# Linear attention feeding a two-layer MLP on one core: moving the key-value products and attention matmuls of batches 1 to 3 within TensorE's order

## The chip, the cores and the metric

One core of a Trainium2 chip runs the whole program. The metric is the device time of one execution in microseconds, as the median of several runs. The profile is one further execution; its span runs from the first to the last instruction of the core, and the device time also holds what lies before and behind that.

## The reference

```python
q_s = exp(q - max(q, axis=-1)) ; q_s = q_s / (sum(q_s, axis=-1) + 1e-09)
k_s = exp(k - max(k, axis=2))  ; k_s = k_s / (sum(k_s, axis=2) + 1e-09)
kv  = einsum('bhsd,bhse->bhde', k_s, v)
x   = einsum('bhsd,bhde->bhse', q_s, kv)      # 8 batches, 8 heads, 576 rows, 64
x   = x.transpose(0, 2, 1, 3).reshape(4608, 512)
h   = x @ w_in                                # 512 -> 2048
out = maximum(0.01 * h, h) @ w_out            # 2048 -> 512
```

q is normalised over the 64 elements of a head, k over the 576 rows; each batch and head has a 64 x 64 product kv. All inputs are float32, each batch's q, k and v 1.18 MB.

## The kernel before

**Two streams of work.** TensorE runs the MLP over the 4,608 tokens in nine tiles t of 512. For every tile, layer 1 computes 16 groups ph (128 hidden features each) of four accumulating matmuls over the four feature blocks of xT, taken in the order 0, 2, 1, 3 (L452). ScalarE turns each ph into gj with the leaky ReLU (L461). Layer 2 then accumulates 16 matmuls over the hidden blocks j into pout, for each of four groups of 128 tokens (L473), and VectorE (in two groups of tile 1 ScalarE) copies pout to out_sb, which SyncE's queue stores. In tile 0 the four groups of tokens run interleaved: four matmuls for j = 0, four for j = 1, and so on, so four pout accumulate at once. In the later tiles one group ends before the next begins.

Between these matmuls stands the attention of the batches that later tiles need. A tile of 512 tokens and a batch of 576 rows do not line up: tile 1 takes the last 64 tokens of batch 0 and the first 448 of batch 1, tile 2 the rest of batch 1 and the first 384 of batch 2.

**Steps of one batch's attention.** k_tree, k_allmax: maximum over rows on VectorE. k_sub: subtract it, on POOL or VectorE (L195). k_exp: exponential on ScalarE into ke (L203). v_cast: v to bfloat16 in vb, in two halves, on ScalarE (L213) or POOL (L215). q_max, q_sub, q_exp, q_sum, q_norm: softmax of q into qe (L226 VectorE, L256 POOL, L264 ScalarE, L273 and L280 VectorE). kv: 36 matmuls of 64 rows, in 18 pairs that use the two halves of the array at once, first all of the first pair of heads, then of the second (L295); the first half of them reads the first v_cast, the second half the second. kd_make: reciprocal and two multiplies for each of kv's two PSUM tiles, on VectorE, into the block-diagonal weights kd (L310, L313). q turned: for batches 0 and 1 by TensorE transposes (L389) that ScalarE copies out into qT (q_keep, L404), for later batches by a DMA into qX. attend or attend_x: a matmul of kd with the turned q for one feature block and a part of the tokens (L412, L440), which ScalarE copies into xT (L422, L446).

**What sets the order.** Every engine runs its instructions in the order in which the program issues them. The MLP's loops call run(t, u) at fixed points, and at(t, u, ...) hangs attention steps there; steps at the same point run in the order in which they were hung. In tile 0, unit u from 32 on is layer 2 behind hidden block j = u - 32 (four matmuls). In later tiles u below 16 is layer 1's group u, and u = 16 + 4 tsub + i is layer 2's group tsub behind its matmul j = 4 i + 3, so 19, 23, 27 and 31 are ends of groups. An at with u over 31 counts on into the next tile. Where the last block of a group ends, its stores are issued ahead of the steps hung there.

**PSUM.** Six buffers (psB) are shared by ph, pkv, the transposes and the attends; two more (psO) hold pout. In tile 0 two of the six hold pout2, the third and fourth group of tokens, until their stores. A new tile takes the buffer that was given back first, so it waits for whoever read that buffer last.

**The lines that the change touches**: L582 to L594 hang batch 1's steps in tile 0; plan (L599) sets kvu (L609), the unit of kv and one less than that of kd_make, as o + 25, with o = 27 for batch 3; plan2 (L617) hangs batch 2's steps in tile 1. RA is rows 0 to 3 of the nine that each partition holds, RB rows 4 to 8; H0 and H1 are the head halves; XR splits the nine rows in five and four.

Of the kernel before, what the change touches and what calls it, by code (L numbers as in the profile page):

```python
# [25 lines left out]
def kernel(  # L26
# [9 lines left out]
    nc = tc.nc  # L36
# [49 lines left out]
    RA, RB = slice(0, 4), slice(4, R)  # L86
# [115 lines left out]
    def k_exp(b, hs):  # L202
        nc.scalar.activation(  # L203
            out=st[b]["ke"][:, :, hs].rearrange("p r h d -> p h r d"),
            in_=st[b]["k"][:, hs],
            func=AF.Exp,
        )

    def v_cast(eng, b, gg):
        o = vb2[b % 2][:, :, gg, 0:128].rearrange("p r (h d) -> p h r d", h=2)  # L210
        i = st[b]["v"][:, 2 * gg : 2 * gg + 2]
        if eng is nc.scalar:
            eng.copy(out=o, in_=i)  # L213
        else:
            eng.tensor_copy(out=o, in_=i)  # L215
# [47 lines left out]
    def q_exp(b, rs):  # L263
        nc.scalar.activation(  # L264
            out=st[b]["qe"][:, rs].rearrange("p r h d -> p h r d"),
            in_=st[b]["q"][:, :, rs],
            func=AF.Exp,
        )

    def q_sum(b, rs):  # L270
        n = rs.stop - rs.start
        qsum = small_pool.tile([P, n, HL], FP32, name="qsum")
        nc.vector.reduce_sum(out=qsum, in_=st[b]["qe"][:, rs], axis=AX.X)  # L273
        st[b]["qrec", rs.start] = qrec = small_pool.tile([P, n, HL], FP32, name="qrec")
        nc.vector.reciprocal(out=qrec, in_=qsum)

    def q_norm(b, rs):
        n = rs.stop - rs.start
        qes = st[b]["qe"][:, rs]
        nc.vector.tensor_tensor(  # L280
            out=qes,
            in0=qes,
            in1=st[b]["qrec", rs.start].unsqueeze(3).to_broadcast([P, n, HL, D]),
            op=ALU.mult,
        )


    def kv(b):

        pkv = [psB_pool.tile([P, 2, 130], FP32, name="pkv", tag=BANK_TAG) for _ in range(2)]  # L290
        for gg in range(2):
            for r in range(R):
                for hh in range(2):
                    rows = slice(hh * L, (hh + 1) * L)
                    nc.tensor.matmul(  # L295
                        pkv[hh][:, gg, 0:129],
                        lhsT=st[b]["ke"][rows, r, 2 * gg : 2 * gg + 2].rearrange(
                            "p h d -> p (h d)"
                        ),
                        rhs=vb2[b % 2][rows, r, gg, 0:129],  # L300
                        start=(r == 0),
                        stop=(r == R - 1),
                    )
        st[b]["pkv"] = pkv

    def kd_make(b):
        for hh in range(2):
            pkv = st[b]["pkv"][hh]
            krec = small_pool.tile([P, 2, 1], FP32, name="krec")
            nc.vector.reciprocal(out=krec, in_=pkv[:, :, 128:129])  # L310
            for hp in range(2):
                p0 = hp * D
                nc.vector.tensor_tensor(  # L313
                    out=kd2[b % 2][p0 : p0 + D, 2 * hh : 2 * hh + 2, p0 : p0 + D],
                    in0=pkv[p0 : p0 + D, :, p0 : p0 + D],
                    in1=krec[p0 : p0 + D].to_broadcast([D, 2, D]),
                    op=ALU.mult,
                )
# [66 lines left out]
    def q_transpose(b, r0, n):  # L385
        ps = psB_pool.tile([P, NB, n, L], BF16, name="psum_qt", tag=BANK_TAG)
        for rr in range(n):
            for gg in range(2):
                nc.tensor.matmul(  # L389
                    ps[:, gg::2, rr],  # L390
                    lhsT=st[b]["qe"][:, r0 + rr, 2 * gg : 2 * gg + 2].rearrange(
                        "p h d -> p (h d)"
                    ),
                    rhs=ident,
                    is_transpose=True,
                    start=(rr == 0 and gg == 0),
                    stop=(rr == n - 1 and gg == 1),
                )
        st[b]["ps", r0] = ps

    def q_keep(eng, b, r0, n, gs=slice(0, 4)):
        o, i = st[b]["qT"][:, gs, r0 : r0 + n], st[b]["ps", r0][:, gs]
        if eng is nc.scalar:
            eng.copy(out=o, in_=i)  # L404
        else:
            eng.tensor_copy(out=o, in_=i)

    def attend(b, gs, c0, n, eng):

        ps = psB_pool.tile([P, len(gs), n], FP32, name="po", tag=BANK_TAG)  # L410
        for i, g in enumerate(gs):
            nc.tensor.matmul(  # L412
                ps[:, i],
                lhsT=kd2[b % 2][:, g],
                rhs=st[b]["qT"][:, g].rearrange("c r l -> c (r l)")[:, c0 : c0 + n],
                start=True,
                stop=True,
            )
        step = gs[-1] - gs[0] if len(gs) == 2 else 1
        o = xT[:, gs[0] : gs[-1] + 1 : step, b * S + c0 : b * S + c0 + n]  # L420
        if eng is nc.scalar:
            eng.copy(out=o, in_=ps)  # L422
        else:
            eng.tensor_copy(out=o, in_=ps)  # L424
# [59 lines left out]
    def at(t, u, *fns):  # L484
        while t > 0 and u >= 32:
            t, u = t + 1, u - 32
        hooks.setdefault((t, u), []).extend(fns)
# [3 lines left out]
            fn()  # L491

    H0, H1 = slice(0, 2), slice(2, 4)

    def load_all(b):
        whole = [(ALLH, ALLR)]
        st[b]["k"] = load(k, b, "k_raw", whole)
        st[b]["q"] = load(q, b, "q_raw", whole)
        st[b]["v"] = load(v, b, "v_raw", whole)
# [80 lines left out]
    at(0, 15, lambda: q_max(1, RA), lambda: q_sub(nc.gpsimd, 1, RA))  # L580
    at(0, 15, lambda: q_max(1, RB), lambda: q_sub(nc.gpsimd, 1, RB))
    at(0, 29, lambda: k_exp(1, H1))  # L582
    at(0, 31, lambda: k_exp(1, H0), lambda: v_cast(nc.scalar, 1, 0))
    at(0, 33, lambda: q_exp(1, RA), lambda: q_sum(1, RA), lambda: q_norm(1, RA))
    at(0, 33, lambda: v_cast(nc.scalar, 1, 1), lambda: q_exp(1, RB))
    at(0, 38, lambda: kv(1), lambda: kd_make(1), lambda: q_sum(1, RB), lambda: q_norm(1, RB))
    at(0, 41, lambda: q_transpose(1, 0, 2), lambda: q_keep(nc.scalar, 1, 0, 2))
    at(0, 42, lambda: q_transpose(1, 2, 2), lambda: q_keep(nc.scalar, 1, 2, 2))
    at(0, 45, lambda: q_transpose(1, 4, 3), lambda: q_keep(nc.scalar, 1, 4, 3))
    at(0, 46, lambda: q_transpose(1, 7, 2), lambda: q_keep(nc.scalar, 1, 7, 2))  # L590
    for i in range(8):
        at(0, 47, lambda i=i: attend(1, [i // 2], 288 * (i % 2), 288, nc.scalar))


    XR = (slice(0, 5), slice(5, R))
# [3 lines left out]
    def plan(b, o):  # L599
        t = b - 2  # L600
        at(t, o, lambda: k_begin(b), lambda: q_begin(b), lambda: k_tree(b, ALLH))
        at(t, o + 3, lambda: k_allmax(b), lambda: k_sub(nc.gpsimd, b, ALLH))
        at(t, o + 7, lambda: q_max(b, ALLR), lambda: q_sub(nc.gpsimd, b, ALLR))
        at(t, o + 11, lambda: k_exp(b, ALLH))
        at(t, o + 12, lambda: v_cast(nc.gpsimd, b, 0), lambda: v_cast(nc.gpsimd, b, 1))
        at(t, o + 16, lambda: q_exp(b, ALLR))
        at(t, o + 18, lambda: q_sum(b, ALLR))
        at(t, o + 21, lambda: q_norm(b, ALLR))
        kvu, pu = o + 25, o + (33 if b == 3 else 34)  # L609
        at(t, kvu, lambda: kv(b))  # L610
        at(t, kvu + 1, lambda: kd_make(b))
        at(t, o + 22, lambda: q_turn(b))
        for i in range(8):
            at(t, pu + i // 2, lambda i=i: attend_x(b, i // 2, XR[i % 2], nc.scalar))


    def plan2():  # L617
        b = 2
        at(1, 0, lambda: k_begin(b), lambda: q_begin(b), lambda: k_tree(b, ALLH))
        at(1, 3, lambda: k_allmax(b))  # L620
        at(1, 6, lambda: k_sub(nc.vector, b, H0), lambda: k_sub(nc.vector, b, H1))
        at(1, 9, lambda: k_exp(b, ALLH))
        for rs in XR:
            at(1, 9, lambda rs=rs: q_max(b, rs), lambda rs=rs: q_sub(nc.gpsimd, b, rs))
        at(1, 13, lambda: v_cast(nc.gpsimd, b, 0), lambda: v_cast(nc.gpsimd, b, 1))
        for i, rs in enumerate(XR):
            at(1, (13, 16)[i], lambda rs=rs: q_exp(b, rs), lambda rs=rs: q_sum(b, rs), lambda rs=rs: q_norm(b, rs))
            at(1, (15, 17)[i], lambda rs=rs: q_turn(b, rs))
        at(1, 21, lambda: kv(b))
        at(1, 22, lambda: kd_make(b))  # L630
        for i in range(8):
            at(1, 28 + i // 2, lambda i=i: attend_x(b, i % 4, XR[i // 4], nc.scalar))

    plan2()
    for b in range(3, B):
# [89 lines left out]
```

## Time and profile before

| | us |
|---|---|
| median of the runs shown | 297.52 |
| other runs shown | 296.36 and 1044.59 |
| span of the profiled execution | 293.0 |
| TensorE matmuls busy in it | 278.8 |
| of these layer 1 (L452) and layer 2 (L473) | 127.1 and 129.1 |
| kv (L295), attends (L412, L440), transposes (L389) | 8.5, 3.4 + 9.8, 3.2 |
| ScalarE, VectorE, POOL busy | 150.8, 144.9, 85.6 |

Busy times of matmuls overlap, since a matmul is counted until its result is out while the next has long begun; the distance from start to start says more. A row of the timeline gives the start, the length, the engine, the line, the operation, the tiles and the count of a run of equal instructions; what stands in square brackets is the time that the engine had no instruction before it, and what ended that. PEld are weight loads, one ahead of each matmul. A few per cent of the matmul records are missing from a trace: here layer 2 has 592 weight loads and 580 matmuls, layer 1 640 and 626. The granted TensorE clock is 0.998 of full speed over the span.

### The profile page before, as it was taken

How to read it: one execution, taken by the hardware profiler on the slowest of the kernel's cores; microseconds unless marked ns; L12 is line 12 of the kernel's file. 1: busy time of each engine (PE TensorE's matmuls, PEld its weight loads, DVE VectorE, ACT ScalarE, POOL GpSimd, SP SyncE). 2: the span in 40 equal slices, each digit the busy share in tenths (PEclk: the TensorE clock that was granted, in tenths of full speed). 3: DMA queues.
4: the chain of work that ended last, by engine and by line, in shares of the span. 5: the costliest groups of instructions: out<-in, count | busy, mean ns of one | idle time of the engine just before them, and what ended most of it. 6: DMA issues, size and time to landing. Idle time of an engine off the chain costs nothing.

```text
span 293.0 us, 4255 instructions
## 1 busy us (share of the span) xinstructions
PE 278.8 (95%) x1634; PEld 139.1 (47%) x1661; DVE 144.9 (49%) x240; ACT 150.8 (51%) x272; POOL 85.6 (29%) x61
## 2 busy tenths in 40 slices
PE   6596999999999999999999999999999999999995
PEld 2265845444544455454445544544455444444443
DVE  3947957885491597189367455735440200110011
ACT  4956682777058605951695338532854066007500
POOL 4645280025029307802920292029300000000000
PEclk9999999999999999999999999999999999999999
DMA  7999999694729553874399138923141310131032
GB/s 258 307 211 387 247 191 400 160 345 152 135 55 326 196 116 91 273 266 88 70 326 276 36 72 289 294 55 72 38 81 38 72 36 1 38 72 36 0 72 73
DMA packets 36580, 45.76 MB, mean 156 GB/s; under 512 B 15952, under 2 KB 19280, under 8 KB 36560
## 3 DMA queue, kind: packets, MB, share of 16 engines
q1 hardware_dynamic: 33120, 41.16, 47.4%
q0 software_dynamic: 3280, 4.20, 8.2%
q8 instruction: 13, 0.21, 0.3%
q10 hardware_dynamic: 160, 0.13, 0.1%
q14 instruction: 7, 0.06, 0.1%
HBM read 36.70 MB, written 9.44 MB: 157 GB/s over the span
## 4 chain that ended last, share of the span: by engine, by line
PE 84%; DMA 3%; DVE 3%; ACT 2%; POOL 2%; issue 1%; POOLq 0%; ACTq 0%
PE pout L473 40%; PE ph L452 39%; DMA w_in_sb<-in_moe_w_in_dram 3%; PE pkv L295 3%; PE po L440 2%; POOL k_raw L195 1%; DVE t L162 1%; ACT vb L213 1%; DVE k_raw L356 1%; ACT xT L422 1%; PE psum_qt L389 1%; POOL w_in_sb L133 0%; ACT qe L264 0%; DVE xT L424 0%; DVE m L179 0%
## 5 line engine op out<-in xcount | busy, mean ns | idle before, releaser
L452 PE MATMUL ph<-xT,w_in_sb 128*128 128x512 bf16 (+1 forms) x626 | 127.1, 357 | 4.3 <-DMA w_in_sb<-in_moe_w_in_dram 1.9
L473 PE MATMUL pout<-w_out_sb,gj 128*128 128x512 bf16 (+2 forms) x580 | 129.1, 373 | 0.9 <-issue 0.5
L461 ACT ACTIVATE gj<-ph 128x512 bf16<-128x512 f32 x144 | 82.5, 604 | 58.5 <-PE ph L452 57.9
L452 PEld LDWEIGHTS <-w_in_sb 128*128 128x128 bf16 x640 | 62.0, 98 | 66.1 <-issue 5.5
L473 PEld LDWEIGHTS <-gj 128*128 128x128 bf16 x592 | 56.9, 98 | 61.6
L467 DVE COPY out_sb<-pout 128x512 f32<-128x512 f32 (+1 forms) x34 | 22.7, 675 | 90.7 <-PE pout L473 82.1
L195 POOL TENSOR_TENSOR k_raw<-k_raw,kall 128x2304 f32<-128x2304 f32 (+1 forms) x6 | 29.1, 4844 | 86.2 <-DVE kall L187 55.8
L273 DVE TENSOR_REDUCE qsum<-qe 128x36 f32<-128x2304 bf16 (+4 forms) x11 | 19.8, 1800 | 39.5 <-ACT qe L264 39.5
L256 POOL TENSOR_TENSOR q_raw<-q_raw,qmax 128x2304 f32<-128x2304 f32 (+4 forms) x11 | 31.1, 2839 | 23.5 <-DVE qmax L226 23.5
L446 ACT CAST xT<-po 128x320 bf16<-128x320 f32 (+1 forms) x48 | 16.8, 402 | 40.0 <-PE po L440 40.0
L203 ACT ACTIVATE ke<-k_raw 128x2304 bf16<-128x2304 f32 (+2 forms) x11 | 17.5, 1595 | 9.7 <-POOL k_raw L195 9.4
L280 DVE TENSOR_TENSOR qe<-qe,qrec 128x2304 bf16<-128x2304 bf16 (+4 forms) x12 | 21.1, 1758 | 0.4
L226 DVE TENSOR_REDUCE qmax<-q_raw 128x36 f32<-128x2304 f32 (+4 forms) x11 | 19.4, 1788 | 0.0
L264 ACT ACTIVATE qe<-q_raw 128x2304 bf16<-128x2304 f32 (+4 forms) x11 | 16.9, 1535 | 0.0
L215 POOL CAST vb<-v_raw 128x1152 bf16<-128x1152 f32 x12 | 13.4, 1151 | 0.0
L467 ACT COPY out_sb<-pout 128x512 f32<-128x512 f32 (+1 forms) x3 | 1.6, 549 | 17.5 <-PE pout L473 17.5
L162 DVE TENSOR_TENSOR t<-k_raw 128x1024 f32<-128x1024 f32 (+1 forms) x10 | 10.1, 1010 | 0.4 <-DMA k_raw<-in_k_dram 0.2
L324 PE MATMUL pout<-zero 128*128 128x512 bf16 x26 | 8.9, 469 | 1.4 <-POOL zero L101 1.3
L162 DVE TENSOR_TENSOR t<-t 128x256 f32<-128x256 f32 (+2 forms) x20 | 9.6, 478 | 0.7
L440 PE MATMUL po<-qX,kd 128*128 128x320 bf16 (+1 forms) x48 | 9.8, 286 | 0.1
L295 PEld LDWEIGHTS <-ke 64*128 64x128 bf16 x252 | 7.2, 93 | 3.2 <-ACT gj L461 1.7
L295 PE MATMUL pkv<-vb,ke 64*128 64x129 bf16 x252 | 8.5, 216 | 0.1
(55 smaller groups left out, 103.5 us busy)
## 6 DMA issues: line engine op xcount, KB each, us to landing
out_dram<-out_sb SPq DMA_DIRECT2D x70, 128.0 KB, 2.4
q_raw<-in_q_dram SPq DMA_DIRECT2D x7, 1152.0 KB, 8.2
v_raw<-in_v_dram SPq DMA_DIRECT2D x7, 1152.0 KB, 11.0
k_raw<-in_k_dram SPq DMA_DIRECT2D x6, 1152.0 KB, 5.8
k_raw<-in_k_dram SPq DMA_DIRECT2D x4, 576.0 KB, 5.6
w_in_sb<-in_moe_w_in_dram POOLq DMA_DIRECT2D x8, 256.0 KB, 7.4
w_out_sb<-in_moe_w_out_dram POOLq DMA_DIRECT2D x3, 512.0 KB, 12.2
v_raw<-in_v_dram SPq DMA_DIRECT2D x2, 576.0 KB, 7.4
```

The lines of the kernel that those rows point to most:

```text
L162: nc.vector.tensor_tensor(out=o, in0=i0, in1=i1, op=ALU.max)
L195: eng.tensor_tensor(out=ks, in0=ks, in1=st[b]["kall"][:, hs].unsqueeze(2).to_broadcast([P, n, R, D]), op=ALU.subtract,)
L203: nc.scalar.activation(out=st[b]["ke"][:, :, hs].rearrange("p r h d -> p h r d"), in_=st[b]["k"][:, hs], func=AF.Exp,)
L226: nc.vector.tensor_reduce(out=m, in_=st[b]["q"][:, :, rs], axis=AX.X, op=ALU.max)
L256: eng.tensor_tensor(out=qs, in0=qs, in1=st[b]["qmax", rs.start].unsqueeze(3).to_broadcast([P, HL, n, D]), op=ALU.subtract,)
L273: nc.vector.reduce_sum(out=qsum, in_=st[b]["qe"][:, rs], axis=AX.X)
L280: nc.vector.tensor_tensor(out=qes, in0=qes, in1=st[b]["qrec", rs.start].unsqueeze(3).to_broadcast([P, n, HL, D]), op=ALU.mult,)
L295: nc.tensor.matmul(pkv[hh][:, gg, 0:129], lhsT=st[b]["ke"][rows, r, 2 * gg : 2 * gg + 2].rearrange("p h d -> p (h d)"), rhs=vb2[b % 2][row ...
L452: nc.tensor.matmul(ph, lhsT=w_in_sb[:, cb, j * P : (j + 1) * P], rhs=xT[:, cb, c0 : c0 + n], start=(i == 0 and first), stop=(i == NB - 1 a ...
L461: nc.scalar.activation(out=o, in_=ph, func=AF.Prelu, alpha=LEAKY_SLOPE)
L467: copy(out=out_sb, in_=pout)
L473: nc.tensor.matmul(pout, lhsT=g_sb[j // 2][:, j % 2, tsub * P : (tsub + 1) * P], rhs=w_out_sb[:, j, os], start=(j == 0), stop=(j == NF - 1),)
```

## The change

Batch 1 (tile 0): kv and kd_make move from unit 38 to unit 41, directly ahead of the transposes; the first v_cast goes ahead of the second half of k_exp on ScalarE; q_sum and q_norm of RB go ahead of kd_make on VectorE; the four transposes gather at units 41 and 43 (from 41, 42, 45 and 46); the eight attends, all at unit 47 so far, go to units 45 (two), 46 (three) and 47 (three), with feature blocks in the order 0, 2, 1, 3. Batch 2 (tile 1): kv moves from unit 21 to 23, the end of a layer-2 group, kd_make from 22 to 24; the attends take the order 0, 2, 1, 3. Batch 3: kv moves from unit 20 of tile 2 to unit 19, the end of a group, and kd_make from 21 to 20. No instruction is added or taken away.

```diff
+    GS = (0, 2, 1, 3)
...
     at(0, 29, lambda: k_exp(1, H1))
-    at(0, 31, lambda: k_exp(1, H0), lambda: v_cast(nc.scalar, 1, 0))
+    at(0, 31, lambda: v_cast(nc.scalar, 1, 0), lambda: k_exp(1, H0))
     at(0, 33, lambda: q_exp(1, RA), lambda: q_sum(1, RA), lambda: q_norm(1, RA))
-    at(0, 33, lambda: v_cast(nc.scalar, 1, 1), lambda: q_exp(1, RB))
-    at(0, 38, lambda: kv(1), lambda: kd_make(1), lambda: q_sum(1, RB), lambda: q_norm(1, RB))
-    at(0, 41, lambda: q_transpose(1, 0, 2), lambda: q_keep(nc.scalar, 1, 0, 2))
-    at(0, 42, lambda: q_transpose(1, 2, 2), lambda: q_keep(nc.scalar, 1, 2, 2))
-    at(0, 45, lambda: q_transpose(1, 4, 3), lambda: q_keep(nc.scalar, 1, 4, 3))
-    at(0, 46, lambda: q_transpose(1, 7, 2), lambda: q_keep(nc.scalar, 1, 7, 2))
+    at(0, 33, lambda: v_cast(nc.scalar, 1, 1), lambda: q_exp(1, RB), lambda: q_sum(1, RB))
+    at(0, 41, lambda: kv(1))
+    at(0, 41, lambda: q_norm(1, RB), lambda: kd_make(1))
+    for r0 in (0, 2):
+        at(0, 41, lambda r0=r0: q_transpose(1, r0, 2), lambda r0=r0: q_keep(nc.scalar, 1, r0, 2))
+    for r0, n in ((4, 3), (7, 2)):
+        at(0, 43, lambda r0=r0, n=n: q_transpose(1, r0, n), lambda r0=r0, n=n: q_keep(nc.scalar, 1, r0, n))
     for i in range(8):
-        at(0, 47, lambda i=i: attend(1, [i // 2], 288 * (i % 2), 288, nc.scalar))
+        at(0, (45, 45, 46, 46, 46, 47, 47, 47)[i], lambda i=i: attend(1, [GS[i // 2]], 288 * (i % 2), 288, nc.scalar))
...
-        kvu, pu = o + 25, o + (33 if b == 3 else 34)
+        kvu, pu = o + (24 if b == 3 else 25), o + (33 if b == 3 else 34)
...
-        at(1, 21, lambda: kv(b))
-        at(1, 22, lambda: kd_make(b))
+        at(1, 23, lambda: kv(b))
+        at(1, 24, lambda: kd_make(b))
         for i in range(8):
-            at(1, 28 + i // 2, lambda i=i: attend_x(b, i % 4, XR[i // 4], nc.scalar))
+            at(1, 28 + i // 2, lambda i=i: attend_x(b, GS[i % 4], XR[i // 4], nc.scalar))
```

## The prediction

> **What bounds the kernel now.** I read the page first, then the timeline around each place that the diff touches, row by row. The page:
>
> ```profile
> span 293.0 us, 4255 instructions
> ...
> PE 278.8 (95%) x1634; PEld 139.1 (47%) x1661; DVE 144.9 (49%) x240; ACT 150.8 (51%) x272; POOL 85.6 (29%) x61
> ...
> PE 84%; DMA 3%; DVE 3%; ACT 2%; POOL 2%; issue 1%; POOLq 0%; ACTq 0%
> ```
>
> TensorE is the bound: 95% busy, 84% of the chain. The chain's other engines stand almost wholly before 24 us (untouched) or at batch 1 (35 to 55 us). Neither program has more matmuls than the other, so the change can only gain where TensorE now stands still, and lose where it makes it stand. I therefore looked for holes at each moved step. A 128x512 matmul starts every 0.216 us, a transpose every 0.056, a kv pair every 0.056 and a 288-column attend every 0.123 when nothing waits (starts in the timeline).
>
> Batch 1's kv (unit 38), timeline (start, length):
>
> ```profile
> 41.88 1.14 ACT L213 CAST vb<-v_raw 128x1152 bf16<-128x1152 f32 x1
> ...
> 42.28 1.48 PE L295 MATMUL pkv<-vb,ke 64*128 64x129 bf16 x36
> ...
> 43.07 0.51 PEld L295 LDWEIGHTS <-ke 64*128 64x128 bf16 x17 [0.24 <-issue]
> ...
> 43.69 2.27 PEld L473 LDWEIGHTS <-gj 128*128 128x128 bf16 x12
> 43.92 2.54 PE L473 MATMUL pout<-w_out_sb,gj 128*128 128x512 bf16 x11 [0.16 <-issue]
> ```
>
> It takes 1.48, elsewhere 1.20: the second half waits for the second v cast, which ends at 43.02. That hole is 0.28 us and real. The "0.16 <-issue" behind it is not: there are 12 weight loads for 11 matmuls, so one matmul record is missing. The same at batch 2's kv (mid-group) beside batch 4's (at a group's end already):
>
> ```profile
> 73.81 1.20 PE L295 MATMUL pkv<-vb,ke 64*128 64x129 bf16 x36
> ...
> 74.94 0.55 PEld L473 LDWEIGHTS <-gj 128*128 128x128 bf16 x4
> 75.17 0.59 PE L473 MATMUL pout<-w_out_sb,gj 128*128 128x512 bf16 x2 [0.16 <-issue]
> ```
> ```profile
> 128.61 1.20 PE L295 MATMUL pkv<-vb,ke 64*128 64x129 bf16 x36
> ...
> 129.73 0.33 PEld L473 LDWEIGHTS <-gj 128*128 128x128 bf16 x3
> 129.74 0.60 PE L473 MATMUL pout<-w_out_sb,gj 128*128 128x512 bf16 x2
> ```
>
> The first weight load comes 1.13 (74.94-73.81) and 1.12 (129.73-128.61) after kv's start: the same. At batch 4 the matmul starts 0.01 behind its load; at batch 2 the record at about 74.94 is lacking and the one at 75.17 is the second.
>
> Batch 1's attends (all at unit 47) and layer 1 behind them, then batch 2's:
>
> ```profile
> 52.48 1.96 PE L412 MATMUL po<-qT,kd 128*128 128x288 bf16 x8
> ...
> 52.80 2.52 ACT L422 CAST xT<-po 128x288 bf16<-128x288 f32 x8 [0.40 <-PE po L412]
> ...
> 54.28 6.00 PE L452 MATMUL ph<-xT,w_in_sb 128*128 128x512 bf16 x25
> ...
> 55.38 4.63 PEld L452 LDWEIGHTS <-w_in_sb 128*128 128x128 bf16 x22 [0.29 <-issue]
> ```
> ```profile
> 84.56 1.54 PE L452 MATMUL ph<-xT,w_in_sb 128*128 128x512 bf16 x4
> 84.66 0.65 ACT L446 CAST xT<-po 128x256 bf16<-128x256 f32 x2 [0.43 <-PE po L440]
> ...
> 85.08 0.74 PEld L452 LDWEIGHTS <-w_in_sb 128*128 128x128 bf16 x4 [0.42 <-issue]
> ```
>
> Eight attends in a row need eight PSUM evictions on ScalarE (one each 0.29), and layer 1 needs their results. From the first attend (52.48) to the second layer-1 group (55.59) pass 3.11 us; the work is 8 x 0.123 + 4 x 0.216 = 1.84. Hole: 1.27 us. Batch 2: layer 1's second matmul takes feature block 2, evicted last but one; it starts at 85.08, 0.52 after 84.56 in place of 0.22. Hole: 0.30.
>
> **Part by part.**
> Batch 1's kv to unit 41. The last matmul of unit 38 starts at 41.97; 12 more put the last of unit 41 at 44.56, kv 0.31 later at 44.87 (as 41.97 to 42.28). ScalarE does the second v cast after q_exp RA, which waits for POOL (q_sub RA ends 40.65): 40.68, cast 41.64 to 42.78. The wait is gone by 2 us: -0.28. The swap of v cast and k_exp fills ScalarE's wait for POOL (0.84 at 38.81) and costs nothing; kv needs k_exp (40.1) only at 44.87.
>
> Group ends of batches 2 and 3: the entry into kv costs 0.31 from matmul start to kv start in both kinds of place (73.50 to 73.81, 128.30 to 128.61), the exit 0.15. I take 0; read literally, the idle rows would give 0.16 to 0.22 each. Trainium skill, "TensorE: Matmul & The Clock Gate", Part 3: a weight load overlaps a running matmul only where their row groups differ. By that rule, entry and exit of the half-array kv cost the same between any two full-array matmuls, group end or not, so it speaks against a gain here; with the restored records the trace agrees, and its sum would be mine.
> Their inputs: batch 3's kv comes 0.86 earlier (102.2), its v casts end at 97.6 and k_exp at 93.8. Batch 2's kd_make falls 1.7 later, to about 78.4; its first reader is the attend at 81.0, and VectorE has nothing else to do until 80.33.
>
> Ahead of transposes (batch 1): kv's exit into a transpose is not in the trace; kv into another matmul is 0.15 (13.69 to 13.84), into an attend 0.18 (15.81 to 15.99), a transpose into kv 0.24. I take 0.15, bounds -0.05 to +0.1 on it.
>
> New wait. VectorE now does q_sum and q_norm of RB before kd_make, and PSUM has six buffers, two in pout2. In the built program the first transpose of unit 43 takes the buffer of pkv's first half and waits for that half's two kd multiplies. When? q_exp RA 40.68, +1.08 q_sum; its chain to the next instruction takes 1.25 + 0.29 + 1.14 (42.01 to 44.69 before), so q_sum RB starts at 44.45 (its input, q_exp RB, ends 44.24 as before). These rows give the rest:
>
> ```profile
> 44.69 0.16 DVE L310 RECIPROCAL krec<-pkv 128x2 f32<-128x2 f32 x1
> 44.89 0.59 DVE L313 TENSOR_TENSOR kd<-pkv,krec 64x128 bf16<-64x128 f32 x2
> ...
> 46.34 1.49 DVE L273 TENSOR_REDUCE qsum<-qe 128x20 f32<-128x1280 bf16 x1
> ...
> 48.17 1.49 DVE L280 TENSOR_TENSOR qe<-qe,qrec 128x1280 bf16<-128x1280 bf16 x1
> ```
>
> 46.34 to 48.17 is 1.83, q_norm to its successor 1.41, kd's half 0.79 (44.69 to 45.48): 44.45 + 1.83 + 1.41 + 0.79 = 48.48. TensorE: kv's last pair 45.85, transposes 46.00, eight of them 0.45, eight matmuls 1.73: 48.18 wanted, 48.58 possible (0.05 for the semaphore, 0.05 to load). Stall +0.40; bounds 0 (VectorE half a microsecond sooner) and +1.0 (as much later). Queued behind it on TensorE: everything.
>
> Attends over units 45, 46, 47 (2, 3, 3). After the stall unit 45 is at 50.89; qT's last copy ends about 50.4, kd's second half about 49.3. The evictions run beside layer 2: the groups at 50.89, 52.00 and 53.23 wait for nothing. Layer 1 starts at 53.60; in order 0, 2, 1, 3 its third matmul needs the sixth eviction (done 53.96 + 0.05, wanted 54.03) and its fourth the eighth (54.56 + 0.05, wanted 54.25): 0.36 of the 1.27 stay, so -0.91 (bounds -0.6 and -1.27). Output copies, and with them batch 2's k_tree on VectorE, fall some 0.75 later. k_exp of batch 2 stood at 64.05 with its input done at 62.33, so that is covered; without that cover each 0.1 delays ScalarE by as much, behind six PSUM buffers.
>
> Batch 2's attends in order 0, 2, 1, 3: block 2 is there, the third matmul waits for 85.03 + 0.05 in place of 85.00, the fourth ends 0.06 late: hole 0.14 in place of 0.30, -0.15 (bounds 0 and -0.30).
>
> Sum: -0.28 + 0 + 0.40 - 0.91 - 0.15 = -0.94 us; span 292.1. From there TensorE has no wait that this could run into, so it reaches the end. The median shown, 297.52, is 4.5 us above the profiled span, the lowest run, 296.36, 3.4. So 295.4 to 296.6 for the same spread; I name 296.2.
>
> **Rivals.**
> (a) Group ends do save: the idle rows are time. For: "0.16 <-issue" three times, always mid-group. Against: the load counts, and holes of 0.43 every 10.8 us all through the trace, where nothing can wait. Gain 0.94 + 3 x 0.2 = 1.5: 295.6. Chance 7%.
> (b) Slower: the wait of unit 43's transposes for kd_make eats it all. Each microsecond that VectorE comes later costs one; from a stall of 1.34 (kd half at 49.4) the kernel is slower than before. For: two reductions and a multiply now stand ahead of it, with the qT copies and attends behind. Against: all five durations are rows. With 2.0: +0.66, 298.2. Chance 8%.
> (c) The same stall cools the clock: the first nine warm-up matmuls start every 0.43 (half speed) until 5.1 us, so one fall costs some 1.9 us; but after 1.85 us of idleness (6.2 to 8.1) matmuls again start every 0.22. It needs more than 1.85: about 2 + 1.9 - 1.34 = +2.6, 300.1. Chance 2%. The Trainium skill, same page, "Why this matters for your kernels", puts the limit at gaps of about 3 us; no run here shows it.
> (d) No change: the stall and the attends' remains cancel the gain to within 0.3, 297.4. Chance 13%.
> My forecast has 70%.
>
> **Numbers.** 2% is 6 us, about what a measurement of this kernel can tell from no change. All cases lie within it: same 0.96. Faster needs six times the gain; slower needs a mishap three times (c): 0.02 each. The range takes the lowest run less 1.3 (attends and vb gain whole, no stall), 295.1, to the median with case (d) and a little of (b), 297.7.
>
> **What would show it.** kv of batch 1 in 1.20 instead of 1.48 at 44.9; a TensorE hole of about 0.4 ahead of the L389 matmuls near 48.5, released by VectorE's L313; attends in groups of 2, 3, 3 without holes; second layer-1 group of the second tile near 54.8 (55.59 before); batch 2's second layer-1 matmul 0.22 after the first; 36 kv matmuls of batches 2 and 3 still in 1.13 plus the same entry and exit. A span change over 2 us either way would make it wrong.

## The result and the profile after

| | us |
|---|---|
| before, median of 22 runs | 296.10 |
| changed, median of 22 runs | 294.93 (293.68 to 295.61) |
| ratio, 95% interval | 0.996 (0.9944 to 0.9976) |
| span of the profiled execution, before and changed | 293.0 and 293.0 |

The kernel is 0.4% faster, 1.2 us by the medians and 0.7 to 1.7 us by the interval. The forecast change was 0.94 us. The forecast time, 296.2 in a range of 295.1 to 297.7, was nevertheless missed, by 0.2 us below the range: the level that the sum was put on was too high. In every run whose own span is on record, of either kernel and of all variants, the time is 1.72 to 1.85 us above that span. One run of the kernel before took 1044.59 us, which nothing on record explains; without it the median is 296.06.

The two spans are equal although the kernel is faster. The page of the changed kernel says where that goes:

```profile
span 293.0 us, 4282 instructions
...
PEclk9989999999999999999999999999999999999999
```

One slice of the granted clock, the third (14.7 to 22.0 us), is an 8. The timeline of TensorE alone from 13 us on, changed kernel (start, length, operation, count):

```profile
13.21 0.85 PE L365 MATMUL pkv<-vb,ke 64*128 64x129 bf16 x18 [1.45 <-ACT vb L213]
13.99 1.89 PE L324 MATMUL pout<-zero 128*128 128x512 bf16 x4
```

and of the kernel before:

```profile
13.22 0.69 PE L365 MATMUL pkv<-vb,ke 64*128 64x129 bf16 x18 [1.44 <-ACT vb L213]
13.84 1.04 PE L324 MATMUL pout<-zero 128*128 128x512 bf16 x3
```

Both programs are the same there. In the changed kernel's execution the matmuls run at half speed from 13.60 to 17.01 us (the 128x512 matmuls of that stretch start every 0.427 us in place of 0.216). Batch 1's kv starts at 45.84 us; with the same program up to there and a clock that held ("batch 1 alone" below) it starts at 44.87, 0.97 earlier. The view by stage gives the granted clock as the third number from the end, 0.52 here, since its window begins 0.12 us ahead of the half-speed stretch:

```profile
13.47:16.89 3.42, 3.42 (x34) 1.93 (x30) 1.57 (x5) 1.93 (x3) 1.78 (x3) 0.52 1.13 211
```

From 40 us on the two traces compare without it. Changed kernel, batch 1:

```profile
45.84 1.20 PE L295 MATMUL pkv<-vb,ke 64*128 64x129 bf16 x36
...
46.97 0.62 PE L389 MATMUL psum_qt<-ident,qe 128*128 128x128 bf16 x8
47.26 1.49 DVE L280 TENSOR_TENSOR qe<-qe,qrec 128x1280 bf16<-128x1280 bf16 x1
...
47.40 1.07 ACT L404 COPY qT<-psum_qt 128x512 bf16<-128x512 bf16 x2 [2.18 <-PE psum_qt L389]
...
48.87 0.59 DVE L313 TENSOR_TENSOR kd<-pkv,krec 64x128 bf16<-64x128 f32 x2
...
49.61 0.72 PE L389 MATMUL psum_qt<-ident,qe 128*128 128x128 bf16 x10 [0.29 <-DVE kd L313]
...
51.89 0.41 PE L412 MATMUL po<-qT,kd 128*128 128x288 bf16 x2
...
53.00 0.53 PE L412 MATMUL po<-qT,kd 128*128 128x288 bf16 x3
...
54.23 0.53 PE L412 MATMUL po<-qT,kd 128*128 128x288 bf16 x3
...
54.60 0.81 PE L452 MATMUL ph<-xT,w_in_sb 128*128 128x512 bf16 x3
55.61 0.81 PE L452 MATMUL ph<-xT,w_in_sb 128*128 128x512 bf16 x3 [0.20 <-ACT xT L422]
```

kv takes 1.20 in place of 1.48. The transposes of unit 43 wait for L313, kd_make's first half: the matmul ahead of them starts at 48.94, they at 49.61, 0.67 later, of which 0.22 is that matmul's own time and 0.46 the hole (the bracket shows 0.29, since the record of the last matmul reaches into the hole). At 49.16, when TensorE could have started them, q_norm (L280, to 48.75) and ScalarE's copies of the first transposes (L404, to 48.47) were done; kd_make's first half ends at 49.46. The attends stand in three groups without a hole. Layer 1's fourth matmul starts 0.58 after the third: a hole of 0.36. Batch 2, layer 1 of tile 2 behind its attends:

```profile
84.80 1.38 PE L452 MATMUL ph<-xT,w_in_sb 128*128 128x512 bf16 x5
...
85.31 0.10 PEld L452 LDWEIGHTS <-w_in_sb 128*128 128x128 bf16 x1 [0.20 <-issue]
```

Its third matmul comes 0.30 after the second and its fourth 0.27 after the third: holes of 0.08 and 0.06 where there was one of 0.30. Sum over what changed, from single starts: batch 1 from unit 38's last matmul to the second layer-1 group took 13.62 us and takes 12.88 (the changed trace has that matmul at 42.94 and the group at 55.82), batch 2 saves 0.16. Together -0.90; with +0.97 from the clock, +0.07, which is the difference of the spans (292.97 and 293.04).

### The profile page after: what moved, and what is told of

It reads as the page before. It is cut to its first block, busy times and chain, and to the rows that moved or that the text cites. A ratio compares the mean times of both kernels' runs of the same rounds, so it can differ in the third digit from the quotient of the medians.

```text
span 293.0 us, 4282 instructions
## 1 busy us (share of the span) xinstructions
PE 282.1 (96%) x1661; PEld 139.9 (48%) x1661; DVE 145.6 (50%) x240; ACT 150.7 (51%) x272; POOL 85.4 (29%) x61
## 4 chain that ended last, share of the span: by engine, by line
PE 85%; DVE 6%; POOL 2%; ACT 2%; issue 1%; POOLq 0%
PE pout L473 39%; PE ph L452 39%; PE pkv L295 2%; PE po L440 2%; DVE qe L280 1%; DVE qsum L273 1%; POOL k_raw L195 1%; DVE t L162 1%; PE pout L324 1%; PE psum_qt L389 1%; POOL q_raw L256 1%; PE po L412 1%; ACT xT L422 1%; PE pkv L365 1%; ACT qe L264 1%
## 5 line engine op out<-in xcount | busy, mean ns | idle before, releaser
L256 POOL TENSOR_TENSOR q_raw<-q_raw,qmax 128x2304 f32<-128x2304 f32 (+4 forms) x11 | 31.1, 2836 | 25.8 <-DVE qmax L226 25.8
L280 DVE TENSOR_TENSOR qe<-qe,qrec 128x2304 bf16<-128x2304 bf16 (+4 forms) x12 | 21.7, 1807 | 0.4
L324 PE MATMUL pout<-zero 128*128 128x512 bf16 x27 | 10.5, 536 | 1.3 <-POOL zero L101 1.3
L313 DVE TENSOR_TENSOR kd<-pkv,krec 64x128 bf16<-64x128 f32 x28 | 8.1, 289 | 0.7
```

Of the source, the lines that this page charges most:

```text
L256: eng.tensor_tensor(out=qs, in0=qs, in1=st[b]["qmax", rs.start].unsqueeze(3).to_broadcast([P, HL, n, D]), op=ALU.subtract,)
L280: nc.vector.tensor_tensor(out=qes, in0=qes, in1=st[b]["qrec", rs.start].unsqueeze(3).to_broadcast([P, n, HL, D]), op=ALU.mult,)
```

## The experiments

All edits are against the changed kernel unless it says before. Times are medians; "before" in each row is the kernel before on the same chip. "Layer 2" is the time from layer 2's first matmul to its last, start to start, in the profiled execution; it leaves the start out and holds all that the change moves on TensorE. In the kernel before it is 253.16 us, in the changed kernel 252.27.

| | runs | us | before | ratio (95%) | layer 2 |
|---|---|---|---|---|---|
| group ends alone | 1 | 297.47 | 295.14 | | 253.17 |
| batch 1 alone | 1 | 294.04 | 295.14 | | 252.42 |
| one transpose tile | 12 | 293.95 | 295.14 | 0.9963 (0.9941 to 0.9986) | 251.85 |
| attends 3, 4, 1 | 1 | 293.53 | 295.14 | | 251.90 |
| before, more warm-up | 11 | 294.43 | 294.79 | 0.998 (0.9964 to 0.9997) | 253.17 |
| more warm-up | 11 | 293.55 | 294.79 | 0.9949 (0.9933 to 0.9965) | 252.25 |
| one tile and 3, 4, 1 | 12 | 294.10 | 294.79 | 0.9962 (0.9939 to 0.9985) | 251.50 |
| all three | 5 | 292.84 | 294.79 | 0.9928 (0.9903 to 0.9953) | 251.48 |
| v_cast swap undone | 1 | 295.56 | 296.02 | | 252.50 |
| first warm-up row alone | 12 | 294.53 | 296.02 | 0.9963 (0.9943 to 0.9984) | 252.27 |
| second warm-up row alone | 12 | 294.28 | 296.02 | 0.9949 (0.993 to 0.9967) | 252.25 |

A single time says little here, since executions of one kernel lie up to 3 us apart. The kernels with one run are read by their traces. The last column says where the spread arises: the three kernels at 253.16 to 253.17 differ by 3.2 us in their spans (292.5 to 295.7), and the changed kernel agrees with its three warm-up variants to 0.03. What follows layer 2's last matmul takes 3.66 to 3.71 us in all thirteen profiles. So the spread lies ahead of layer 2, and the change is worth 0.89 to 0.92 us behind that point.

**Are the group ends worth anything?** The kernel before with only

```diff
-        kvu, pu = o + 25, o + (33 if b == 3 else 34)
+        kvu, pu = o + (24 if b == 3 else 25), o + (33 if b == 3 else 34)
...
-        at(1, 21, lambda: kv(b))
-        at(1, 22, lambda: kd_make(b))
+        at(1, 23, lambda: kv(b))
+        at(1, 24, lambda: kd_make(b))
```

> The kernel before with only the key-value products of batches 2 and 3 (and their kd_make) moved to the group ends. My theory: nothing, since the 0.16 us of idle behind a mid-group kv is a missing matmul record; from the last matmul ahead of kv to the first attend of its batch the distance is 1.44 us for kv plus 0.216 for each layer-2 matmul, mid-group or not, and the layer-2 loop of tiles 1 and 2 takes as long as before. Rival (the idle rows are time): 0.2 us less for each of the two.

Batch 2's kv and what follows, group ends alone:

```profile
78.25 1.20 PE L295 MATMUL pkv<-vb,ke 64*128 64x129 bf16 x36
79.38 4.49 PE L473 MATMUL pout<-w_out_sb,gj 128*128 128x512 bf16 x19
...
87.28 1.54 PE L452 MATMUL ph<-xT,w_in_sb 128*128 128x512 bf16 x5
```

No idle bracket any more, as hoped, and 19 records for the 20 matmuls between kv and the attends. What decides is a distance with the whole of kv in it. From the fourth layer-1 matmul of tile 1 to the first of tile 2, start to start, it is 29.190 us in the kernel before (55.374 to 84.564) and 29.191 here (58.087 to 87.278). From there to the last matmul ahead of batch 4's kv, which takes in batch 3's, it is 43.734 in both. The group ends are worth nothing, to 0.001 us in this execution. The theory holds, the rival falls. The span of 295.7 is the start's: this execution had two half-speed stretches, from 8.7 and from 25.8 us.

**Batch 1 alone.** Batches 2 and 3 back in their old places and order.

> The changed kernel with batches 2 and 3 put back to their old places and order. My theory: from the last matmul of unit 38 to the second layer-1 group of tile 1 it takes 12.9 us as in the changed kernel (13.6 before), with a hole of 0.46 ahead of unit 43's transposes and 0.36 in layer 1; batch 2's attends leave their old hole of 0.30 in layer 1 of tile 2; kv of batches 2 and 3, mid-group, costs 1.44 plus any matmul whose record is missing. Rival: 1.67 with all matmul records there.

From unit 38's last matmul (41.97) to the second group (54.85) it is 12.88 us, the hole ahead of unit 43's transposes is 0.46, layer 1's 0.36, batch 2's 0.30: all as expected. kv of batches 2 and 3 shows 1.67 from matmul to matmul again, with a record missing once more:

```profile
73.08 1.19 PE L295 MATMUL pkv<-vb,ke 64*128 64x129 bf16 x36
...
74.20 0.76 PEld L473 LDWEIGHTS <-gj 128*128 128x128 bf16 x5
74.43 0.81 PE L473 MATMUL pout<-w_out_sb,gj 128*128 128x512 bf16 x3 [0.16 <-issue]
```

The rival could have pointed to this row; the distances above answer it.

**What does unit 43 wait for?**

```diff
-    for r0 in (0, 2):
-        at(0, 41, lambda r0=r0: q_transpose(1, r0, 2), lambda r0=r0: q_keep(nc.scalar, 1, r0, 2))
+    at(0, 41, lambda: q_transpose(1, 0, 4), lambda: q_keep(nc.scalar, 1, 0, 4))
```

> The changed kernel with the four rows of RA transposed into one PSUM tile and copied out at once, so one PSUM buffer is free for the transposes of unit 43 and only the second of them (4 matmuls) takes the buffer that kd_make frees. My theory (the wait is for the buffer that kd_make's first half gives back): the hole ahead of unit 43's first transpose goes (0.46 to 0), 0.1 us stays ahead of the second, the kernel is 0.35 us faster than the changed one, 0.9957 to 0.993 of the kernel before. Rival (the transposes wait for q_norm of RB or for ScalarE's copies): the hole stays at 0.46.

```profile
48.66 0.59 DVE L313 TENSOR_TENSOR kd<-pkv,krec 64x128 bf16<-64x128 f32 x2
...
48.94 0.76 PE L389 MATMUL psum_qt<-ident,qe 128*128 128x128 bf16 x10
```

The transposes start while kd_make's first half still runs, 0.22 behind the matmul ahead of them: the first hole is gone, and 0.04 is left ahead of the second set (ten transposes take 0.60 in place of 0.56). So it was the buffer that kd_make frees and not q_norm or a copy. From unit 41's last matmul (45.32) to layer 1's fourth (54.98) it is 9.66 us, in the changed kernel 10.08 (45.53 to 55.61): 0.42 less. The times could not show that by themselves: the ratio, 0.9963, lies just above the expected stretch, and its interval holds the changed kernel's 0.996 too. One correction to the section on the kernel belongs here: a new tile does not take the buffer that comes free first in time. In the changed kernel the copies out of the first two transposes were done at 48.47, a microsecond before kd_make's first half, and the next transposes still waited for the latter. In the program kd_make stands ahead of those copies; whether that order decides, or a fixed turn of the buffers, no run here shows.

**What is left of the attends' hole?**

```diff
-        at(0, (45, 45, 46, 46, 46, 47, 47, 47)[i], ...
+        at(0, (45, 45, 45, 46, 46, 46, 46, 47)[i], ...
```

> The changed kernel with the eight attends at units 45 (three), 46 (four) and 47 (one). My theory (what stays of the attends' hole is the eviction of the last attend, behind two others): the hole of 0.36 us in layer 1 of tile 1 falls to 0.05 or less and the attends themselves wait for nothing. Rival (the hole comes from the output copies or from the return to layer 1): it stays at 0.36.

```profile
52.18 0.65 PE L412 MATMUL po<-qT,kd 128*128 128x288 bf16 x4
52.67 1.03 PE L473 MATMUL pout<-w_out_sb,gj 128*128 128x512 bf16 x4
53.53 0.29 PE L412 MATMUL po<-qT,kd 128*128 128x288 bf16 x1
53.65 2.54 PE L452 MATMUL ph<-xT,w_in_sb 128*128 128x512 bf16 x10
```

Layer 1's first groups run without a hole. With one attend directly ahead of layer 1 instead of three, the last eviction is ready in time: the fourth matmul starts 0.22 behind the third (0.58 in the changed kernel).

**Where do the two groups of times come from?** The kernel before, and the changed kernel, with nine more warm-up matmuls:

```diff
-    wake(14)
+    wake(17)
...
     k_all_pe(0, 1)
-    wake(2)
+    wake(8)
```

> The kernel before with nine more warm-up matmuls in the start (three more in the first row of them, six more ahead of the first key-value products), so TensorE stands idle less before 16 us. My theory (the two groups of times, some 1.2 us apart, come from the TensorE clock falling to half for one window of 3.4 us in the start of some executions): the times draw together around the lower group of the kernel before, 294.5 to 295.1. Rival (the spread has nothing to do with the start): the same two groups as before, about 294.8 and 296.2.

> The changed kernel with the same nine warm-up matmuls. My theory: one group of times around 293.9, 0.9 us below the kernel before with the same warm-up matmuls, the change's own effect without the clock. Rival: groups at 293.9 and 295.1 as in the changed kernel.

All times, sorted, in us:

```
before            294.47 294.70 294.81 295.09 295.14 295.48 295.85 295.89 295.92 295.96 296.06 ... 297.52, 1044.59
changed           293.68 293.71 293.78 293.88 293.95 294.01 294.10 294.35 | 294.82 294.82 294.91 ... 295.61
before, warm-up   294.27 294.32 294.36 294.37 294.40 294.43 294.45 294.48 294.51 294.54 294.62
changed, warm-up  293.40 293.46 293.46 293.52 293.52 293.55 293.56 293.57 293.60 293.63 293.71
```

The spread falls from 2 to 3 us to 0.35. Neither profile has a half-speed stretch in the start. The two rows of eleven do not overlap, and their medians lie 0.88 us apart: that is the change without the clock. In the lower groups of the first two rows one reads nearly the same, 294.8 and 293.9.

On the chip of the warm-up runs the kernel before had 23 of its 29 times between 294.49 and 295.03, so eleven times without a straggler would be weak evidence. The mean granted clock of each run is stronger; a stretch of 3.41 us at half speed takes 0.006 off it. All 27 runs with both rows lengthened were granted 0.997 or more. Of the 57 runs of the changed kernel and its three warm-up variants, the 25 granted 0.997 or more took 293.40 to 294.03 us, the 32 granted 0.994 or less 293.95 to 295.90. The groups are therefore not clean: a half-speed stretch can cost almost nothing.

That the rows with more warm-up lie some 0.35 below the old lower groups was not expected. In their profiles layer 1's wait for w_in ends at 23.41 and 23.50 us, in the kernel before and with batch 1 alone, whose clock held too, at 23.89. Why w_in lands earlier is open.

**Do the two remaining holes of batch 1 add up?** One transpose tile and attends 3, 4, 1 together, without and with the warm-up.

> The changed kernel with one PSUM tile for RA's transposes and attends as three, four and one. My theory: both remaining holes of batch 1 (0.46 and 0.36) fall to 0.15 together, so 0.67 us less than the changed kernel, about 0.994 of the kernel before. Rival (one hole hides behind the other, so only the larger counts): 0.45 less.

> The same with the nine warm-up matmuls: all three together. My theory: one group of times around 293.2, 1.6 us below the kernel before with warm-up matmuls, about 0.990 of the kernel before. Rival: the warm-up matmuls delay the first key-value products and it is no faster than without them.

In the trace of the first both holes are gone: 44.57 to 53.87 for the stretch that took 10.08, 9.30, so 0.78 less. By time, without warm-up, the groups hide it (294.10 against 293.55 with warm-up and without these edits). With warm-up it is 292.84 (292.72 to 293.04) against 293.55 (293.40 to 293.71): 0.71 less. The holes add up; the level is lower than expected by the same 0.35 as above. Three things together make the fastest kernel of this study, 1.6 us below the kernel before with the same warm-up and 0.9928 of the kernel before.

**Was the v_cast swap free?**

```diff
-    at(0, 31, lambda: v_cast(nc.scalar, 1, 0), lambda: k_exp(1, H0))
+    at(0, 31, lambda: k_exp(1, H0), lambda: v_cast(nc.scalar, 1, 0))
```

> The changed kernel with the first v_cast behind the second half of k_exp again, as before. My theory (ScalarE has slack there, the later place of kv alone took the wait for the second v_cast away): kv still runs without a hole (1.44 us from matmul to matmul), q_exp RA starts some 0.3 us later, and with it q_sum and q_norm of RA, RB and kd_make on VectorE, so the hole ahead of unit 43's transposes grows from 0.46 to 0.7. Rival (the swap is worth nothing at all): that hole stays at 0.46.

```profile
49.59 0.59 DVE L313 TENSOR_TENSOR kd<-pkv,krec 64x128 bf16<-64x128 f32 x2
...
50.33 0.72 PE L389 MATMUL psum_qt<-ident,qe 128*128 128x128 bf16 x10 [0.53 <-DVE kd L313]
```

kv has no hole without the swap either (1.44 from matmul to matmul), but unit 43's grows from 0.46 to 0.69, as expected. ScalarE's wait for POOL is on the path by way of q_exp, q_sum, q_norm and kd_make, so the swap is worth 0.23 us (252.50 against 252.27 by layer 2), and only because of the new wait.

**Which hole of the start?** Each row of warm-up matmuls by itself.

> The changed kernel with only the first row of warm-up matmuls lengthened, 17 for 14. My theory (a window of 3.4 us in which the array works under some 38% makes the next one half-speed, and the hole at 6.3 to 8.1 us is the one that most windows fail by): most times near 293.7, a minority near 294.9. Rival (only the hole at 11.6 to 13.2 counts): about as many in the upper group as in the changed kernel, six or more in ten.

> The changed kernel with only the second hole filled, eight warm-up matmuls for two ahead of the first key-value products. My theory: a part of the times stays in the upper group near 294.9, more than with the first row lengthened. Rival (only the hole at 11.6 to 13.2 counts): all near 293.6.

With the first row alone six of twelve times lie at 293.6 to 294.0 and six at 295.0 to 295.7; so the upper group is no minority, and the theory's order of the two holes was wrong. With the second row alone nine lie between 293.5 and 294.4, the rest up to 295.9. That is not the rival's picture either, in which the second row alone would have brought all to 293.6. Neither row ends the spread, both together do.

## Why the prediction was right about the change and wrong about the time

| step | forecast | measured |
|---|---|---|
| vb wait at batch 1's kv | -0.28 | -0.30 |
| group ends | 0 | 0.00 |
| kd_make's wait at unit 43 | +0.40 | +0.46 |
| batch 1's attends (hole 1.27) | -0.91 | -0.91 |
| batch 2's attends | -0.15 | -0.16 |
| sum | -0.94 | -0.90 by the traces, -0.88 with the warm-up, -1.17 by the medians |

Each term came from starts, row by row, and each came out within 0.06. The medians' 1.17 holds, beside the change, how many half-speed stretches fell into either set of runs; its interval, 0.7 to 1.7, takes in 0.90. The step from a kv into a transpose, which no row had shown, was taken as 0.15 and is 0.15 (46.82 to 46.97). What the prediction drew from the Trainium skill's rule of row groups stands too: kv costs 1.44 from matmul to matmul wherever it is put. That does not prove the rule. Read literally it does not fit these traces: in layer 1, where all 128 rows are in use, a weight load starts together with the matmul ahead of it (85.510 and 85.509 in the kernel before), and a matmul still starts every 0.216.

The step that failed is the last one of the sum, from the span to the time: "The median shown, 297.52, is 4.5 us above the profiled span, the lowest run, 296.36, 3.4. So 295.4 to 296.6 for the same spread; I name 296.2", and with it the range's foot, the lowest run less 1.3. It took the distance between one execution's span and the times of two others as a term that the changed kernel keeps. The distance between an execution's time and its own span is 1.72 to 1.85 us wherever both are on record. The profiled execution of the kernel before had no half-speed stretch in its start, so the time that belongs to the span of 292.1 is 292.1 + 1.8 = 293.9; the changed kernel's four runs granted 0.998 or more took 293.68 to 293.88. The other 1.6 to 2.7 us of the term were what two slower executions had lost; where, is not on record for these two, but in the traces it is the start. Over 22 runs the kernel before has a median of 296.10 and reaches down to 294.47. That both runs shown lay above the median was bad luck; 296.10 less 0.94 would have been 295.2. The rivals' times do not share one level either: 296.2 and (a) stand on 297.1, (b) and (c) on 297.5.

Rival (c) had a mechanism that exists, in another place and at another price. The clock does fall to half, not at the new wait but in the start, in runs of either kernel. Its condition was wrong: "It needs more than 1.85" was read off one execution in which the clock happened to hold; the changed kernel's clock fell behind a window whose longest hole was 1.6 us (11.6 to 13.2). With the Trainium skill's rule ("TensorE: Matmul & The Clock Gate", "Why this matters for your kernels": no idle gap over about 3 us) one would not have expected it either; here windows whose longest hole was 1.2 to 2.4 us were enough, so the measurement decides against that figure.

The swap of v_cast and k_exp was put at nothing "and costs nothing". It is a small gain that the table's +0.46 already contains: without it that term would be +0.69.

Rivals (a), (b) and (d) fell: no gain from the group ends, no stall that eats the sum, no cancelling.

## What to carry to other kernels

An idle bracket behind an instruction is worth a count of weight loads against matmuls before it is taken for time; a distance between two landmarks with the step in it does not depend on the records. A step that is moved ahead of another takes PSUM buffers with it: look which tile comes round to the buffer, and put small tiles together where a bank holds them. Before a forecast of tenths of a per cent, find out what the level does from run to run, and put a span and a time together only if they come from one execution: here filling TensorE's holes in the start with nine idle matmuls shrank the spread from 2 to 3 us to 0.35 and made a change of 0.3% visible in eleven runs.

## What the runs showed of the hardware that was not expected

The half-speed stretches in the start last 3.41 us each and begin on a grid of 3.41 us counted from the first rise of the clock: eight of them in seven of the thirteen profiles. With the swap undone, for instance, the clock rises at 4.06 us and falls at 14.30, three times 3.41 later. I worked out, from the starts and lengths of the matmul records, in what share of each window of that grid the array worked, for the first 33 us of the thirteen profiles (an estimate: missing records are left out, and a record is taken less the 0.163 us by which a 0.379 us record exceeds the 0.216 from start to start). All seven windows under 0.39 were followed by a window at half speed; of the five between 0.40 and 0.43 one was; of those above none. So a single hole need not fill a window, and a long one need not bring a fall: the longest, 2.88 us with the swap undone, lay across two windows of 0.48 and 0.43, and the clock held behind both.

Where the stretch falls matters. At 13.6 to 17.0 us it put batch 1's kv 0.97 us later (45.84 against 44.87 with batch 1 alone). Stretches at 8.2 to 11.7 (attends 3, 4, 1) and 9.1 to 12.5 (one tile and 3, 4, 1) left it at 44.90 and 44.88, since layer 1 waits for w_in until 23.92 and 23.89 us there, as it does with batch 1 alone (23.89). Yet with a stretch at 9.2 to 12.6 (one transpose tile) that wait lasted to 24.65 and kv came at 45.63. So the landing of w_in moves the level as well, and what moves the landing was not tried. Nor was it tried by itself that the share is the cause; that the warm-up matmuls end the spread was.
